# Second product of the last hidden blocks by seven products of quarters, after the first product

## The chip, the cores and the metric

The kernel runs on one core of one Trainium2 chip. The metric is device microseconds of one execution, the median of several runs; lower is better. A core has TensorE (PE, matmuls, with its weight loads shown apart as PEld), VectorE (DVE), ScalarE (ACT), GpSimd (POOL) and SyncE (SP), which issues most of the DMAs here. Each engine works through its own queue in order and waits on semaphores for the others.

## The reference

A transformer block over 2048 rows of 512 elements, in float32: LayerNorm, attention with 32 heads of 16 over 8 keys at a spacing of 2, an output product and a residual, then LayerNorm and an MLP with 1792 hidden elements and a squared ReLU, and a second residual.

```python
S, D, H, W, dil, F = 2048, 512, 32, 8, 2, 1792
def attention(x):                       # x: [S, D], 16 elements a head
    q, k, v = split_heads(x @ wqkv)
    # row s sees rows s, s-2, ..., s-14
    logits = einsum("hsd,hswd->hsw", q, k_window) * 16 ** -0.5
    return merge_heads(einsum("hsw,hswd->hsd", softmax(masked(logits)), v_window)) @ wo
def mlp(x):
    r = relu(x @ w1 + b1)               # [S, F]
    return (r * r) @ w2 + b2
h = x + attention(layernorm(x))
out = h + mlp(layernorm(h))
```

## The kernel before

**Products in two parts.** Every float32 operand of a matmul is split in a high part (a cast to float32r, `hi`, on ACT) and a low part (the rest, `lo`, a subtraction on DVE or POOL). A product is the sum of three: high by high, low by high, high by low. `mm3` does this for the products ahead of the MLP.

**Passes.** Rows are handled in four groups of 512 (R = 4 tiles of 128). After the products for q, k and v, the MLP runs in four passes u = 0 to 3, one for each group. In the first three the attention and the output product of the next group run beside it on the other engines. The change lies in the last pass, u = 3, which has nothing to run ahead for.

**The last pass before.** The hidden elements are 14 blocks f of 128, taken in seven pairs (`PAIRS`, (2, 9) first and (4, 11) last). The *first product* (r = relu(h w1 + b1), transposed, 128 hidden x 512 rows) is done for a pair by Winograd's form of Strassen's method: seven products of quarters in place of eight, 6 matmuls of 256 columns each. `products_a(n)` issues four of them (24 matmuls), `products_b(n)` three (18); the quarters are summed up in four PSUM banks (`XB`). The sums of w1's quarters come from `t_load(n)` (four DMAs into `traw`), `t_sums(n)` (four additions, on DVE for n < 2, else on POOL) and `t_split(n)` (one cast `th` on ACT, then two low parts `tl`, of w1's rows 256 to 511 first). In `products_b`, product 7 adds into the bank that u of `products_a` was computed from, so it comes after that DVE addition.

Of the result, `rest` and `second` make the squared ReLU of the pair's two blocks, and `squared` splits it into `rh` and `rl`. The *second product* of one block f (`mlp2`, called by `second_product`) is 12 matmuls of 512 columns: four tiles j, three terms, into four accumulators `acc[0..3]`. The high parts of w2 all lie in SBUF; of the low parts, 4 to 6 do, and `fetch` brings others from DRAM as places come free. After the seventh pair the last blocks' second products run tile by tile, `finish` adds the accumulator to the residual h (brought back from DRAM by `unspill`) and stores the tile, and `last_tile` does the last tile in two halves.

**What sets the order.** Everything is written out in program order per engine. The loop over n issues TensorE's work directly; other work is put on lists by `at(delta, fn, ...)`, "in the slot that is delta from now", and run by `end_slot` in the order in which it was put there. Each n has two slots, one after `products_a` and its second product, one after `products_b`. Row tiles of [128, 512] come from one tag with 15 buffers.

Of the kernel before, what the change touches and what calls it, by code (L numbers as in the profile page):

```python
# [20 lines left out]
RI = 2  # L21
# [9 lines left out]
LAG = 3  # L31
# [27 lines left out]
def block_kernel(ctx, tc, x, wqkv, wo, w1, b1, w2, b2, out):  # L59
    nc = tc.nc  # L60
# [20 lines left out]
    out_v = out.rearrange("o (b p i e) d -> (o b) e i p d", b=2, p=P, i=R, e=2)  # L81
# [26 lines left out]
    due = {}  # L108
# [4 lines left out]
    def at(delta, fn, *a):  # L113
        due.setdefault(now["slot"] + delta, []).append((fn, a))
# [7 lines left out]
    def end_slot(pe):  # L122
        now["pe"] += pe
        run(due)
        pump()
        run(amid)
        run(late)
        now["slot"] += 1

    def run(chores):  # L130
        todo = chores.get(now["slot"], [])
        while todo:
            fn, a = todo.pop(0)
            fn(*a)
# [16 lines left out]
    def hi(dst, src):  # L151
        nc.scalar.copy(dst, src)  # L152

    def lo(eng, dst, src, h):
        eng.tensor_tensor(out=dst, in0=src, in1=h, op=ALU.subtract)  # L155
# [438 lines left out]
    hs, hn = {}, {}  # L594
# [199 lines left out]
    def t_load(n):  # L794
        f = PAIRS[n][0]
        tw[n] = t_tile(n, "traw")
        for k in range(KB):
            nc.sync.dma_start(tw[n][:, k], bass.AP(
                tensor=w1.tensor, offset=w1.offset + k * P * F + f * P,
                ap=[[F, P], [F // 2, 2], [1, P]]))  # L800
# [39 lines left out]
    HD = D // 2  # L840
    pairs = {}

    def products_a(n):
        b = {m: psum.tile([P, D], F32, name="mm", tag=tag)[:, :HD]
             for m, tag in zip((1, 4, 2, 3), XB)}
        pu = row("p"), row("u")
        pairs[n] = b, pu
        for m, bank in ((1, 1), (4, 4), (6, 2), (5, 3)) if not n else ((1, 1), (6, 2), (5, 3), (4, 4)):
            product(n, m, b[bank], True, m == 4)
        nc.scalar.copy(pu[0][:, :HD], b[1])  # L850
        if not n:
# [3 lines left out]
        nc.vector.tensor_tensor(out=pu[1][:, :HD], in0=b[2], in1=pu[0][:, :HD], op=ALU.add)
        nc.scalar.copy(pu[0][:, HD:], b[3])

    def products_b(n):
        b, (p, u) = pairs[n]
        f, g = PAIRS[n]  # L860
        for m, bank in ((2, 1), (7, 2), (3, 3)):
            product(n, m, b[bank], False, True)
        rf, rg = row("r"), row("r")
        pairs[n] = rg
        tt = nc.vector.tensor_tensor
        nc.scalar.activation(rf[:, :HD], b[1], AF.Relu, bias=b1_sb[:, f:f + 1])
        tt(out=u[:, HD:], in0=b[2], in1=p[:, :HD], op=ALU.add)
        tt(out=rf[:, HD:], in0=u[:, HD:], in1=b[4], op=ALU.subtract)
        nc.gpsimd.tensor_tensor(out=rg[:, HD:], in0=u[:, HD:], in1=p[:, HD:], op=ALU.add)
# [10 lines left out]
        squared(g, rg)  # L880

    def squared(f, r):
        rh, rl = work.tile([P, D], F32R, name="rh", bufs=LAG + 1), row("rl", dt=F32R)
        nc.scalar.activation(r, r, AF.Square)
# [28 lines left out]
    def mlp2(u, f, acc, js, first=False, last=False, mid=None):  # L913

        rh, rl = hid[u, f]
        terms = [(rh, w2_h, j) for j in js] + [(rh, w2_l, j) for j in js]
        if len(js) > 1:
            terms += [(rl, w2_h, j) for j in js]
        else:
            terms.insert(1, (rl, w2_h, js[0]))  # L920
        for n, (l, w, j) in enumerate(terms):
            if mid and n == len(terms) // 2:
                mid()
            nc.tensor.matmul(acc[j], l[:, j * P:(j + 1) * P], w[f],  # L924
                             start=(first and n < len(js)),
                             stop=(last and n >= len(terms) - len(js)))
# [9 lines left out]
    def last_tile(t, fs):  # L936


        u, i = divmod(t, R)
        b, e = divmod(u, 2)  # L940
        h = hs.pop(t)
        js = slice(i * P, (i + 1) * P)
        for c, eng in ((slice(0, D // 2), nc.sync), (slice(D // 2, D), nc.scalar)):
            ps = turn["tr"].tile("half")[:, :D // 2]
            terms = [(f, l, w) for f in fs for l, w in ((0, w2_h), (1, w2_h), (0, w2_l))]
            for n, (f, l, w) in enumerate(terms):
                nc.tensor.matmul(ps, hid[u, f][l][:, js], w[f][:, c], start=(n == 0),  # L947
                                 stop=(n == len(terms) - 1))
            nc.vector.tensor_tensor(out=h[:, c], in0=ps, in1=h[:, c], op=ALU.add)  # L949
            eng.dma_start(out_v[b, e, i, :, c], h[:, c])  # L950
# [148 lines left out]
    place = {}  # L1099
# [121 lines left out]
    def second_product(last=False):  # L1221
        q = used[0]
        f = fs[q]
        if last:
            mlp2(u, f, acc, js[:-1])
            mlp2(u, f, acc, js[-1:], False, True)
        else:
            mlp2(u, f, acc, js, q == 0)
        used[0] += 1
# [29 lines left out]

    h = hs[S // P - 1]  # L1260
    for j in js[:-1]:
        for f in fs[-2:]:
            mlp2(u, f, acc, [j], False, f == fs[-1])
            if j == 0:
                end_slot(0.65)
        at(0, finish, R * u + j, acc[j])
        if j == 1:
            at(0, nc.vector.tensor_tensor, h, acc[-1], h, ALU.add)
        if j:
            run(due)  # L1270
# [24 lines left out]
```

## Time and profile before

| | |
|---|---|
| median of three runs | 501.18 us (501.14 to 502.29) |
| the profiled execution | 500.91 us, span 499.1 us |
| busy: PE, PEld | 99%, 84% |
| busy: DVE, ACT | 77%, 61% |
| instructions: PE, DVE, ACT, POOL | 2411, 526, 543, 429 |
| last pass, first matmul to last | 421.88 to 495.92 us in the span |
| granted clock of TensorE | 1.000 |

The profile's rows have the line of the kernel, the engine, the operation, `out<-in` by the program's names and the shapes. In the timeline the first two numbers are start and length in us, and in brackets stands the idle time of the engine before the instruction, with what ended it. A row may cover several instructions (xN). Matmuls overlap: a matmul's length is longer than the spacing of two. In the chain of work that ended last, a row has the start and length of a stretch of the chain.

### The profile page before, as it was taken

The numbers are of one execution on the slowest core, as the hardware profiler recorded it, in microseconds if no ns is written. First come the engines' busy times: TensorE is split into PE (matmuls) and PEld (weight loads), VectorE is DVE, ScalarE is ACT, GpSimd is POOL, SyncE is SP. The second block draws the span as 40 slices with busy tenths as digits, with TensorE's granted clock in tenths as the row PEclk, the third lists the DMA queues.
The fourth block names the chain that finished last, engine by engine and source line by source line (L and its number), as shares of the span: only waits on it lengthen the run. The fifth ranks groups of instructions, "written<-read, shape, count | busy, mean of one in ns | idle before, by whom it ended". The sixth has DMA issues, their size and how long they took to land.

```text
span 499.1 us, 7514 instructions
## 1 busy us (share of the span) xinstructions
PE 494.2 (99%) x2411; PEld 420.6 (84%) x2411; DVE 383.7 (77%) x526; ACT 305.7 (61%) x543; POOL 354.6 (71%) x429
## 2 busy tenths in 40 slices
PE   8999999999999999999999999999999999999997
PEld 7998888888888888888888888888888888998986
DVE  6479899999989989998979989897984257733233
ACT  4634778668346757478564556866454968766551
POOL 5714798996775999888878777787889353885610
PEclk9999999999999999999999999999999999999999
DMA  8779979889788899689776945977680575355212
GB/s 269 201 215 244 281 253 297 272 268 310 209 219 260 294 286 259 185 226 248 219 253 210 218 143 164 269 236 258 201 202 14 130 193 163 117 158 169 64 42 87
DMA packets 113584, 103.67 MB, mean 208 GB/s; under 512 B 33672, under 2 KB 82056, under 8 KB 113544
## 3 DMA queue, kind: packets, MB, share of 16 engines
q1 hardware_dynamic: 112600, 102.66, 70.1%
q10 hardware_dynamic: 944, 0.52, 0.3%
q8 instruction: 19, 0.31, 0.3%
q14 instruction: 21, 0.17, 0.1%
HBM read 72.65 MB, written 24.25 MB: 194 GB/s over the span
## 4 chain that ended last, share of the span: by engine, by line
PE 98%; DMA 1%; ACT 0%; ACTq 0%; DVE 0%; issue 0%
PE mm L231 49%; PE acc L924 30%; PE wo L231 9%; PE mm L837 7%; PE tr L204 2%; DMA wraw<-in_A_wqkv_dram 1%; PE half L947 0%; ACTq L570 0%; ACT big_h L152 0%; ACT xh L152 0%; DVE h L949 0%
## 5 line engine op out<-in xcount | busy, mean ns | idle before, releaser
L414 POOL TENSOR_TENSOR pr<-pr 128x512 f32<-128x512 f32 (+1 forms) x128 | 134.1, 1048 | 35.6 <-DVE pr L357 30.2
L231 PE MATMUL mm<-big_l,w_h 128*128 128x512 f32 x336 | 88.5, 390 | 0.0
L357 DVE TENSOR_TENSOR pr<-ex,v 128x1024 f32<-128x1024 f32 x62 | 75.6, 1221 | 12.0 <-POOL o L414 9.2
L344 DVE TENSOR_TENSOR pr<-qp,k 128x1024 f32<-128x1024 f32 x64 | 76.8, 1200 | 6.1 <-ACT qp L271 3.3
L380 DVE TENSOR_REDUCE ex<-pr 128x64 f32<-128x1024 f32 x64 | 78.4, 1225 | 1.8
L231 PEld LDWEIGHTS mm<-big_l,w_h 128*128 128x128 f32 x336 | 63.0, 188 | 13.4 <-ACT r L894 0.3
L155 POOL TENSOR_TENSOR rl<-r,rh 128x512 fp32r<-128x512 f32 x42 | 54.9, 1306 | 24.2 <-ACT rh L152 20.1
L231 PE MATMUL mm<-big_l,xh 128*128 128x512 f32 (+1 forms) x208 | 56.3, 379 | 0.0
L231 PE MATMUL mm<-big_h,xh 128*128 128x512 f32 (+1 forms) x208 | 53.1, 377 | 0.3 <-ACT xh L152 0.3
L231 PE MATMUL mm<-big_h,xl 128*128 128x512 f32 (+1 forms) x208 | 52.6, 374 | 0.0
L924 PE MATMUL acc<-big_h,rh 128*128 128x512 f32 x190 | 52.1, 391 | 0.0
L924 PE MATMUL acc<-big_l,rh 128*128 128x512 f32 x190 | 52.0, 390 | 0.0
L924 PE MATMUL acc<-big_h,rl 128*128 128x512 f32 x190 | 51.7, 390 | 0.0
L231 PE MATMUL mm<-big_l,w_l 128*128 128x512 f32 x168 | 44.9, 389 | 0.0
L231 PEld LDWEIGHTS mm<-big_h,xl 128*128 128x128 f32 x208 | 38.3, 188 | 6.0
L231 PEld LDWEIGHTS mm<-big_h,xh 128*128 128x128 f32 x208 | 37.9, 188 | 6.1 <-ACT xh L152 0.5
L924 PEld LDWEIGHTS acc<-big_h,rl 128*128 128x128 f32 x190 | 35.7, 188 | 7.4
L924 PEld LDWEIGHTS acc<-big_l,rh 128*128 128x128 f32 x190 | 35.6, 188 | 7.4
L231 PEld LDWEIGHTS mm<-big_l,xh 128*128 128x128 f32 x208 | 37.4, 188 | 4.9
L924 PEld LDWEIGHTS acc<-big_h,rh 128*128 128x128 f32 x190 | 35.1, 188 | 7.1 <-DVE h L932 0.3
L894 ACT ACTIVATE r<-mm,b_sb 128x512 f32<-128x512 f32 x42 | 28.7, 684 | 16.2 <-PE mm L231 15.7
L231 PEld LDWEIGHTS mm<-big_l,w_l 128*128 128x128 f32 x168 | 31.5, 188 | 6.6
(167 smaller groups left out, 919.4 us busy)
## 6 DMA issues: line engine op xcount, KB each, us to landing
k<-qkv_d SPq DMA_DIRECT2D x50, 288.0 KB, 3.2
v<-qkv_d SPq DMA_DIRECT2D x46, 288.0 KB, 3.2
qkv_d<-y SPq DMA_DIRECT2D x18, 512.0 KB, 4.0
big_l<-w2l_d SPq DMA_DIRECT2D x24, 256.0 KB, 3.1
xt<-in_A_x_dram SPq DMA_DIRECT2D x16, 256.0 KB, 4.2
q<-qkv_d SPq DMA_DIRECT2D x32, 128.0 KB, 3.6
h<-in_A_x_dram SPq DMA_DIRECT2D x16, 256.0 KB, 3.3
h_d<-h SPq DMA_DIRECT2D x16, 256.0 KB, 3.4
```

The lines of the kernel that those rows point to most:

```text
L155: eng.tensor_tensor(out=dst, in0=src, in1=h, op=ALU.subtract)
L204: nc.tensor.transpose(tr[:, k, :], src[:, k * P:(k + 1) * P], ident)
L231: nc.tensor.matmul(ps, l(k), r(k), start=(n == 0), stop=(n == 3 * KB - 1))
L344: nc.vector.tensor_tensor(out=pr.rearrange("p i w h d -> p i w (h d)"), in0=qps["now"][:, j % 2].unsqueeze(2).to_broadcast([P, RI, W, GC]) ...
L357: nc.vector.tensor_tensor(out=p2, in1=vwin, op=ALU.mult, in0=e1[:, :, :, j * GH:(j + 1) * GH].unsqueeze(4).to_broadcast([P, RI, W, GH, DH]))
L380: nc.vector.tensor_reduce(out=lf[:, :, :, j * GH:(j + 1) * GH], in_=pr, axis=X, op=ALU.add)
L414: nc.gpsimd.tensor_tensor(out=dst, in0=p2[:, :, :w], in1=p2[:, :, w:2 * w], op=ALU.add)
L837: nc.tensor.matmul(ps, sta[y][:, k], mov[x][:, k], start=(first and q == 0), stop=(last and q == len(terms) - 1), skip_group_check=True)
L894: nc.scalar.activation(r, ps, AF.Relu, bias=b1_sb[:, f:f + 1])
L924: nc.tensor.matmul(acc[j], l[:, j * P:(j + 1) * P], w[f], start=(first and n < len(js)), stop=(last and n >= len(terms) - len(js)))
```

## The change

The last three pairs, (0, 7), (1, 8) and (4, 11), are taken out of the second product's row of blocks, and their second product is also done by seven products of quarters. For each pair the stationary side is r (2 blocks of hidden elements by two halves of the rows) and the moving side w2 (2 blocks by two halves of the columns). This needs:

- sums of w2's quarters: `v_load(q)` loads the two blocks of w2 again, as `vraw`; `v_sums(q)` makes four sums (DVE for q = 0 and 1, POOL for q = 2); `v_split(q)` makes two casts and two low parts. Loads are issued in n = 1, 2 and 4 (`VS`), the sums in the second slot of the same n, the split in the second slot of the next;
- sums of r's quarters: `s_sums(n)` (four on DVE), `s_split(n)` (two casts on ACT, two low parts on DVE);
- all parts of r in the last pass now lie in columns of w1's parts that their own pair has used, not in tiles of their own (`parted`).

The eight other blocks keep their wide second product, one in each n from 1 to 6, one more in n = 5 (`PLAN`, first number: after `products_a`, second: after `products_b`), and one after the last `products_b`. Then come `outer(n)` for the three pairs (products 1, 6, 5, 7, into the four banks of the first product), and `inner` (product 4 into the left halves of `acc[2]` and `acc[3]`); products 3 and 2 of tiles 0 and 1 come last, and the last half tile goes into a bank of its own, `z`. The four outer results are summed up on ACT and DVE and added to h by POOL and DVE beside these. The `unspill` loads move from n = 4 and 5 to behind the first `outer`.

```diff
+WN = 3
+PLAN = {1: (1, 0), 2: (1, 0), 3: (1, 0), 4: (1, 0), 5: (1, 1), 6: (1, 0)}
+VS = {1: 0, 2: 1, 4: 2}
+VP = range(2)
...
-        rh, rl = work.tile([P, D], F32R, name="rh", bufs=LAG + 1), row("rl", dt=F32R)
         nc.scalar.activation(r, r, AF.Square)
-        hi(rh, r)
-        lo(nc.vector, rl, r, rh)
-        hid[R - 1, f] = rh, rl
+        rh, rl = [w[:, :, f * P:(f + 1) * P] for w in (w1_h, w1_l)]
+        parted(f, r)
+    def parted(f, r):
+        rh, rl = [w[:, :, f * P:(f + 1) * P] for w in (w1_h, w1_l)]
+        n = RI if f in WINO[:WN] else R
+        src = r.rearrange("p (j c) -> p j c", j=R)[:, :n]
+        hi(rh[:, :n], src)
+        lo(nc.vector, rl[:, :n], src, rh[:, :n])
+        hid[R - 1, f] = [lambda j, a=a: a[:, j] for a in (rh, rl)]
+    def v_sums(q):
+        (b11, b12), (b21, b22) = [(r[:, :HD], r[:, HD:]) for r in vw[q]]
+        tt, sub = (nc.vector if q in VP else nc.gpsimd).tensor_tensor, ALU.subtract
+        tt(out=b11, in0=b12, in1=b11, op=sub)
+        tt(out=b12, in0=b22, in1=b12, op=sub)
+        tt(out=b22, in0=b22, in1=b11, op=sub)
+        tt(out=b21, in0=b21, in1=b22, op=sub)
+    def s_split(n):
+        for x, f in zip(whole.pop(n), PAIRS[n - PLAIN]):
+            src = x.rearrange("p (j c) -> p j c", j=R)
+            h, l = [w[:, :, f * P:(f + 1) * P] for w in (w1_h, w1_l)]
+            hi(h, src)
+            lo(nc.vector, l, src, h)
+    def part(n, m, ps, js, first=False, last=False):
...
+        terms = [(x, y, j) for x, y in ((0, 0), (1, 0), (0, 1)) for j in js]
+        for k, (x, y, j) in enumerate(terms):
+            nc.tensor.matmul(ps[j], sta[x][:, i0 + j], mov[y], start=first and k == 0,
+                             stop=last and k >= len(terms) - len(js), skip_group_check=True)
...
     for n in range(len(PAIRS)):
         if n + 2 < len(PAIRS):
             t_load(n + 2)
+        if n in VS:
+            v_load(VS[n])
         products_a(n)
...
             at(0, second, n - 1)
+            if n > PLAIN:
+                at(0, s_sums, n - 1)
             if n + 1 < len(PAIRS):
                 at(0, t_split, n + 1)
-            second_product()
-        if n in (4, 5):
-            for i in range(2):
-                at(0, unspill, R * u + 2 * (n - 4) + i)
+            for _ in range(PLAN[n][0]):
+                second_product()
         end_slot(5.6)
         products_b(n)
         if n + 2 < len(PAIRS):
             at(0, t_sums, n + 2)
-        if n > 1:
+        if n in VS:
+            at(0, v_sums, VS[n])
+            at(2, v_split, VS[n])
+        if n > PLAIN:
+            at(0, s_split, n - 1)
+        for _ in range(PLAN[n][1] if n else 0):
             second_product()
         if n == len(PAIRS) - 1:
             at(0, second, n)
-            second_product(True)
+            at(0, s_sums, n)
+            at(0, s_split, n)
+            for i in js:
+                at(1, unspill, R * u + i)
+            while used[0] < len(fs):
+                second_product()
         end_slot(4.9)
...
-    last_tile(S // P - 1, fs[-2:])
+    for n in range(head, end):
+        outer(n)
+    inner(head, 4)
+    outer(end)
+    tt = nc.vector.tensor_tensor
+    v, u2, u3, s12, s22 = [row("c") for _ in range(5)]
+    nc.scalar.copy(v, two[1])
+    tt(out=u2, in0=two[6], in1=v, op=ALU.add)
...
+    for eng, i, cs, src in ((nc.gpsimd, 0, left, v), (nc.gpsimd, 1, left, v),
+                            (nc.gpsimd, 2, left, u3), (nc.gpsimd, 3, left, u3),
+                            (nc.vector, 2, right, s22), (nc.vector, 3, right, s22),
+                            (nc.gpsimd, 0, right, s12), (nc.gpsimd, 1, right, s12)):
...
+    for n in range(head + 1, end + 1):
+        inner(n, 4)
+    for i in (2, 3):
+        finish(R * u + i, acc[i])
+    z = psum.tile([P, D], F32, name="part", tag=XB[0])[:, left]
+    for m, j, ps in ((3, 0, acc[0][:, right]), (2, 0, acc[0][:, left]),
+                     (3, 1, acc[1][:, right]), (2, 1, z)):
+        for n in range(head, end + 1):
+            part(n, m, [ps, ps], [j], ps is z and n == head, n == end)
+        if m == 2 and not j:
+            finish(R * u, acc[0])
...
+    tt(out=h, in0=acc[1], in1=h, op=ALU.add)
+    nc.scalar.dma_start(out_v[b, e, 1, :, right], h[:, right])
+    tt(out=h[:, left], in0=z, in1=h[:, left], op=ALU.add)
+    nc.sync.dma_start(out_v[b, e, 1, :, left], h[:, left])
```

Here `PLAIN` is 4, the number of pairs left to the wide second product, `head` is 4 and `end` is 6, and `WINO` lists the last three pairs' first blocks, then their second ones.

More of the change, by code (lines that the diff above doesn't have):

```diff
@@ L865, in products_b @@
         tt = nc.vector.tensor_tensor
+        if n >= PLAIN:
+            whole[n] = rf, rg
         nc.scalar.activation(rf[:, :HD], b[1], AF.Relu, bias=b1_sb[:, f:f + 1])
@@ new lines, in block_kernel, with v_load @@
+    hid = {}
+    PLAIN = len(PAIRS) - WN
+    WINO = [p[i] for i in range(2) for p in PAIRS[PLAIN:]]
+    whole, vw = {}, {}
+    def v_load(q):
+        vw[q] = row("vraw"), row("vraw")
+        for r, f in zip(vw[q], PAIRS[PLAIN + q]):
+            nc.sync.dma_start(r, w2[f * P:(f + 1) * P, :])
+    def v_sums(q):
[5 more added lines that the diff above has]
+        tt(out=b21, in0=b21, in1=b22, op=sub)
@@ new lines, in v_split @@
+    def v_split(q):
+        if q == 0:
+            t = [work.tile([P, D], F32R, name="rh", bufs=LAG + 1) for _ in range(4)]
+        elif q == 1:
+            t = [att.tile([P, D], F32R, name="vs", tag=tag) for tag in ("k", "k", "v", "v")]
+        else:
+            t = [a[:, i] for a in [att.tile([P, 2, D], F32R, name="vs", tag="o", bufs=3)
+                                   for _ in range(2)] for i in range(2)]
+        raw = vw[q]
+        vw[q] = t[:2], t[2:]
+        for i in range(2):
+            hi(t[i], raw[i])
+            lo(nc.vector, t[2 + i], raw[i], t[i])
@@ new lines, in s_sums @@
+    def s_sums(n):
+        rf, rg = whole.pop(n)
+        (a11, a21), (a12, a22) = [(r[:, :HD], r[:, HD:]) for r in (rf, rg)]
+        x = whole[n] = row("x"), row("x")
+        tt, sub = nc.vector.tensor_tensor, ALU.subtract
+        tt(out=x[0][:, :HD], in0=a21, in1=a22, op=ALU.add)
+        tt(out=x[1][:, :HD], in0=a11, in1=a21, op=sub)
+        tt(out=x[0][:, HD:], in0=x[0][:, :HD], in1=a11, op=sub)
+        tt(out=x[1][:, HD:], in0=a12, in1=x[0][:, HD:], op=sub)
+    def s_split(n):
[4 more added lines that the diff above has]
+            lo(nc.vector, l, src, h)
@@ new lines, in part @@
+    def part(n, m, ps, js, first=False, last=False):
+        q, (f, g) = n - PLAIN, PAIRS[n]
+        c, d = PAIRS[q]
+        col, i0 = {1: (f, 0), 2: (g, 0), 4: (g, 2), 5: (c, 0), 6: (c, 2), 7: (d, 0), 3: (d, 2)}[m]
+        sta = [w[:, :, col * P:(col + 1) * P] for w in (w1_h, w1_l)]
+        lo_, hi_ = slice(0, HD), slice(HD, D)
+        if m < 4:
+            w, cs = f if m == 1 else g, hi_ if m == 3 else lo_
+            mov = w2_h[w][:, cs], w2_l[w][:, cs]
+        else:
+            i, cs = {5: (0, lo_), 7: (0, hi_), 4: (1, lo_), 6: (1, hi_)}[m]
+            mov = [t[i][:, cs] for t in vw[q]]
+        terms = [(x, y, j) for x, y in ((0, 0), (1, 0), (0, 1)) for j in js]
+        for k, (x, y, j) in enumerate(terms):
+            nc.tensor.matmul(ps[j], sta[x][:, i0 + j], mov[y], start=first and k == 0,
+                             stop=last and k >= len(terms) - len(js), skip_group_check=True)
@@ L896, in hidden @@
         hi(rh, r)
-        at(wait, lo, nc.vector if u == R - 1 else nc.gpsimd, rl, r, rh)
-        hid[u, f] = rh, rl
+        at(wait, lo, nc.gpsimd, rl, r, rh)
+        hid[u, f] = [lambda j, a=a: a[:, j * P:(j + 1) * P] for a in (rh, rl)]
     def hidden_now():
@@ L923, in mlp2 @@
                 mid()
-            nc.tensor.matmul(acc[j], l[:, j * P:(j + 1) * P], w[f],
+            nc.tensor.matmul(acc[j], l(j), w[f],
                              start=(first and n < len(js)),
@@ L934, in finish @@
         nc.sync.dma_start(out_v[b, e, i], h)
[L936 to L950, printed above, removed]
     def flush():
@@ L1213, in block_kernel @@
     now["sub"] = u
-    fs = [f for pair_ in PAIRS for f in pair_]
-    need = [f for f in fs if f < 12 and f not in place]
+    fs = [f for pair_ in PAIRS[:PLAIN] for f in pair_]
+    need = [f for f in fs + WINO if f < 12 and f not in place]
     acc = [psum.tile([P, D], F32, name="acc", tag=tag) for tag in ("acc0", "acc1", "tr0", "tr1")]
@@ L1219, in block_kernel, with refill @@
     used = [0]
[L1221 to L1229, printed above, removed]
+    def refill(f):
         if f < 12 and need:
@@ L1232, in second_product @@
             at(1, fetch, need.pop(0))
+    def second_product():
+        q = used[0]
+        mlp2(u, fs[q], acc, js, q == 0, q == len(fs) - 1)
+        used[0] += 1
+        refill(fs[q])
     for n in range(len(PAIRS)):
@@ L1256, in block_kernel @@
             at(0, second, n)
-            second_product(True)
-        end_slot(4.9)
[L1260 to L1270, printed above, removed]
-    last_tile(S // P - 1, fs[-2:])
+            at(0, s_sums, n)
@@ new lines, in block_kernel, with outer @@
+            at(0, s_split, n)
[3 more added lines that the diff above has]
+                second_product()
+        end_slot(4.9)
+    two = {m: psum.tile([P, D], F32, name="part", tag=tag) for m, tag in zip((1, 5, 6, 7), XB)}
+    halves = {m: [t[:, j * HD:(j + 1) * HD] for j in range(RI)] for m, t in two.items()}
+    both, left, right = range(RI), slice(0, HD), slice(HD, D)
+    head, end = PLAIN, len(PAIRS) - 1
+    def outer(n):
+        for m in (1, 6, 5, 7) if n < end else (1, 6, 7, 5):
+            part(n, m, halves[m], both, n == head, n == end)
+        refill(PAIRS[n][0])
+        run(due)
+        now["slot"] += 1
@@ new lines, in inner @@
+    def inner(n, m):
+        part(n, m, [acc[RI + j][:, left] for j in both], both, False, n == end)
+    for n in range(head, end):
[6 more added lines that the diff above has]
+    tt(out=u2, in0=two[6], in1=v, op=ALU.add)
+    tt(out=u3, in0=two[7], in1=u2, op=ALU.add)
+    tt(out=s22, in0=two[5], in1=u3, op=ALU.add)
+    tt(out=s12, in0=two[5], in1=u2, op=ALU.add)
@@ new lines, in block_kernel @@
+    for eng, i, cs, src in ((nc.gpsimd, 0, left, v), (nc.gpsimd, 1, left, v),
+                            (nc.gpsimd, 2, left, u3), (nc.gpsimd, 3, left, u3),
+                            (nc.vector, 2, right, s22), (nc.vector, 3, right, s22),
+                            (nc.gpsimd, 0, right, s12), (nc.gpsimd, 1, right, s12)):
+        h = hs[R * u + i][:, cs]
+        eng.tensor_tensor(out=h, in0=h, in1=src[:, i % RI * HD:(i % RI + 1) * HD], op=ALU.add)
+    for n in range(head + 1, end + 1):
+        inner(n, 4)
@@ new lines, in block_kernel @@
+    for i in (2, 3):
[7 more added lines that the diff above has]
+            finish(R * u, acc[0])
+    h = hs.pop(R * u + 1)
+    b, e = divmod(u, 2)
+    tt(out=h, in0=acc[1], in1=h, op=ALU.add)
```

## Prediction

> **What bounds the kernel now.** I read the page's totals first, then the chain of work that ended last over the final pass, then the timeline of each queue in that pass, and last the groups of instructions by form. n is the index of a pair in `PAIRS`, "a(n)" and "b(n)" are the 24 and 18 matmuls of `products_a` and `products_b`, "m7" is product 7.
>
> ```profile
> span 499.1 us, 7514 instructions
> PE 494.2 (99%) x2411; PEld 420.6 (84%) x2411; DVE 383.7 (77%) x526; ACT 305.7 (61%) x543; POOL 354.6 (71%) x429
> ...
> PE 98%; DMA 1%; ACT 0%; ACTq 0%; DVE 0%; issue 0%
> ```
>
> TensorE is the bound, POOL has the next longest queue beside it in this pass, and the chain never leaves TensorE there:
>
> ```profile
> 440.71 2.15 PE mm L837 x18
> 442.87 2.75 PE acc L924 x12
> 445.61 2.87 PE mm L837 x24
> ...
> 484.94 9.55 PE acc L924 x42
> 494.49 1.44 PE half L947 x12
> ...
> 495.96 0.42 DVE h L949
> ```
>
> From here come my prices: 18 or 24 matmuls of 256 columns take 2.15 or 2.87 us, 0.1195 each; the 12 of 512 columns of one second product take 2.75, the step between widths included. So a saving in matmuls is a saving in time, as long as TensorE still finds every operand ready. Before, each pair's 42 narrow matmuls have two second products beside them (10.5 us a pair); afterwards pairs 2, 3 and 4 have one: 5.02 + 2.75 = 7.77 us. So I looked for the work that must end once per pair, and where it was late already:
>
> ```profile
> 434.25 0.33 SPq L697 DMA_DIRECT2D h_d<-h  x1
> 434.67 2.53 SPq L798 DMA_DIRECT2D traw<-in_B_w_dram  x4
> 437.30 0.54 SPq L697 DMA_DIRECT2D h_d<-h  x1
> ```
> ```profile
> 438.18 0.85 POOL L805 TENSOR_TENSOR traw<-traw 128x256 f32<-128x256 f32 x1 [0.30 <-DMA traw<-in_B_w_dram]
> 439.49 0.74 POOL L806 TENSOR_TENSOR traw<-traw 128x256 f32<-128x256 f32 x1 [0.46 <-DMA traw<-in_B_w_dram]
> 440.31 1.06 POOL L807 TENSOR_TENSOR traw<-traw 128x256 f32<-128x256 f32 x1
> 441.45 0.74 POOL L808 TENSOR_TENSOR traw<-traw 128x256 f32<-128x256 f32 x1
> 443.35 2.56 POOL L155 TENSOR_TENSOR tl<-traw,th 128x512 fp32r<-128x512 f32 x2 [1.16 <-ACT th L152]
> 445.85 1.20 POOL L869 TENSOR_TENSOR r<-u,p 128x256 f32<-128x256 f32 x1
> 447.01 0.74 POOL L805 TENSOR_TENSOR traw<-traw 128x256 f32<-128x256 f32 x1
> ...
> 449.47 0.74 POOL L808 TENSOR_TENSOR traw<-traw 128x256 f32<-128x256 f32 x1
> 451.37 2.55 POOL L155 TENSOR_TENSOR tl<-traw,th 128x512 fp32r<-128x512 f32 x2 [1.16 <-ACT th L152]
> 453.88 0.74 POOL L869 TENSOR_TENSOR r<-u,p 128x256 f32<-128x256 f32 x1
> ```
> ```profile
> 442.22 1.05 ACT L152 CAST th<-traw 128x1024 fp32r<-128x1024 f32 x1 [2.27 <-DMA traw<-in_B_w_dram]
> ```
>
> The reader is to see POOL's round for one pair: four sums of the raw quarters (`t_sums`), a wait for ACT's cast `th`, two low parts `tl`, then one addition of the pair before. From the end of `tl` of pair 3 (443.35 + 2.56 = 445.91) to that of pair 4 (451.37 + 2.55 = 453.92) it takes 8.01 us. Against 10.5 us of TensorE it is hidden; against 7.77 it is the longer one. And pair 3 starts late: its raw weights leave SP only at 434.67, behind a spill, and POOL waits for them twice.
>
> **The change part by part.**
>
> *TensorE.* The second product of six hidden blocks, 72 wide matmuls, becomes 7 products x 6 narrow x 3 pairs = 126. Before, ten second products stand ahead of the end of b(6), and 11.14 us follow it (484.78 to 495.92, the last matmul's end): 10 x 2.75 + 11.14 = 38.64. After: seven ahead, one behind, and 126 x 0.1195 = 15.06, with 0.16 for the last one's drain: 8 x 2.75 + 15.22 = 37.22. Saved: 1.4 us. This is all that can be gained; `last_tile` went into it.
>
> *The end.* As before, a 256-column addition and one 128 KB store follow the last matmul; cost 0. The eight additions into h, four sums of `two` and four `finish`-like additions lie beside the last 7.2 us of matmuls (42 in outer(6) and both late inners, 36 after them): POOL has six of about 0.74 (its row L869, 453.88), done some 4.5 us after product 1 of outer(6), 1.7 before the addition to tile 1 wants the last. Cost 0, a microsecond if that cover fails.
>
> *Pair 3 comes sooner.* The second product between b(2) and a(3) is gone. These rows give the places:
>
> ```profile
> 440.55 0.40 PE L837 MATMUL mm<-big_l,w_h 128*128 128x256 f32 x2
> ...
> 441.26 0.40 PE L837 MATMUL mm<-wo_h,th 128*128 128x256 f32 x2
> ...
> 442.70 1.09 PE L924 MATMUL acc<-big_h,rh 128*128 128x512 f32 x4
> ```
> ```profile
> 466.49 0.40 PE L837 MATMUL mm<-big_l,w_h 128*128 128x256 f32 x2
> ...
> 468.16 0.40 PE L837 MATMUL mm<-wo_h,tl 128*128 128x256 f32 x2
> ```
>
> b(2) starts at 440.55 with the same work ahead of it in both kernels. a(3) would follow at 442.70 and reach the second `tl` 1.67 later (466.49 to 468.16), at 444.37. POOL delivers it at 445.91: at least 1.54 us of standstill, by rows that nothing in the change makes earlier.
>
> *`v_load(0)` and `v_sums(0)`.* Its two loads stand in SP's queue behind `traw` of pair 3 (434.67 + 2.53 = 437.20), ahead of the spill, a fetch of w2's low part and `traw` of pair 4. Its sums stand on DVE ahead of u of pair 2, and m7 of b(2) writes over the bank that u reads.
>
> ```profile
> big_l<-w2l_d SPq DMA_DIRECT2D x8, 256.0 KB, 2.9
> ```
> ```profile
> 438.36 0.41 DVE L855 TENSOR_TENSOR u<-mm,p 128x256 f32<-128x256 f32 x1
> 440.04 0.73 DVE L155 TENSOR_TENSOR rl<-r,rh 128x512 fp32r<-128x512 f32 x1 [1.28 <-POOL traw L805]
> ```
> ```profile
> L784 DVE TENSOR_TENSOR s<-pl 128x256 f32<-128x256 f32 x2 | 0.8, 418 | 0.0
> L884 ACT ACTIVATE r<-r 128x512 f32<-128x512 f32 x14 | 8.9, 633 | 0.4
> L152 ACT CAST rh<-r 128x512 fp32r<-128x512 f32 x14 | 8.7, 621 | 0.4
> L155 DVE TENSOR_TENSOR rl<-r,rh 128x512 fp32r<-128x512 f32 x14 | 11.3, 807 | 23.7 <-ACT rh L152 19.0 <-POOL traw L808 2.6 <-POOL traw L805 1.3
> ```
>
> Issued at 437.2 and 437.6, landed 2.9 later, 440.1 and 440.5; four sums of 0.42 end near 442.2, u near 442.65 instead of 438.77. m7, due at 441.26 (the second row above), starts near 442.7, 1.4 late. The other delay runs through POOL: its addition at 440.31 took 1.06 and not 0.74 while DVE's op of 440.04 ran (0.73, in the rows ahead), 0.32 more; by that share four DVE sums add about 0.2 each, less the 0.32 already there: `tl` ends at about 446.4. The two delays overlap: 446.4 + 0.1 - 444.37 = 2.1 us. Bounds: 1.54, and 2.9 if the loads land 0.8 later in a queue that is moving data all that time. I take 2.1.
>
> The Trainium skill, page "SBUF — State Buffer", section "Who interferes with whom", says that a DVE instruction with two SBUF inputs and a GpSimd instruction that reads SBUF exclude each other, the later one standing still until the first is done. The trace agrees in direction: 1.06 for 0.74, though 0.32 is less than DVE's whole 0.73.
>
> *Pairs 4 and 5.* After pair 3 TensorE and POOL leave together, so each pair costs the difference of their rounds: 8.01 - 7.77 = 0.24 as a floor. Pair 4's round has `v_sums(1)` beside it, up to 4 x 0.2: 0.24 to 1.0; I take 0.6, because some of these fall where POOL waits for `th` (its 1.16 us). Pair 5's has the two low parts of `v_split(1)`, up to 2 x 0.32: 0.24 to 0.9, taken 0.5. ACT's additions (`v_split`, 2 x 0.62 a pair) come before `th` in its queue. The row of pair 3's stretch before, whose columns are TensorE, weight loads, DVE, ACT and POOL:
>
> ```profile
> 445.42:455.94 10.52, 10.52 (x67) 9.54 (x66) 3.80 (x7) 5.91 (x10) 9.05 (x11) 1.00 0.37 113
> ```
>
> ACT gets to 5.91 + 1.24 = 7.15 of 7.77 us and stays inside; POOL, with 9.05 busy, does not.
>
> *Pair 6.* `PLAN[5]` leaves two second products: TensorE's round is 10.52. POOL loses the wait for `th` but gets `v_sums(2)`, four more at 0.82 from start to start (447.01 to 449.47 is three): 8.01 - 1.16 + 3.28 = 10.13, and up to 0.8 from `s_sums(4)` on DVE: 0 to 0.4, taken 0.1.
>
> *The parts of r behind the first product.* Removed: `rl`'s rows. Added a pair: 1.5 more casts and low parts, four sums. After b(6) the order is `rest(6)`, `s_split(5)`, `second(6)`, `s_sums(6)`, `s_split(6)`. By the rows above: eight ACT operations of 0.63 (5.0), a low part 0.7, four sums 1.7, a cast 0.6 and two low parts 1.4: the last near 9.4 us after b(6). TensorE has one second product, two outers and an inner, 2.75 + 2 x 2.87 + 0.72 = 9.2, and wants the last part 1.44 later, at 10.65. Hidden, by 1.2; up to 1 us if pair 6 leaves ACT behind. That r's parts go into columns of w1 costs 0 as well: product 3 has read those columns by then, and a cast into one part of a weight tile holds no matmul on its other parts, as at the kernel's start, where both are `big_h`:
>
> ```profile
> 16.02 0.93 ACT L152 CAST big_h<-wraw 128x384 fp32r<-128x384 f32 x2
> 16.48 0.85 PE L231 MATMUL mm<-big_h,xl 128*128 128x384 f32 x4
> ```
>
> If it did hold them, each of 13 handovers would cost a cast and a low part, some 1.4 us; I give that no chance of its own. The four moved `unspill` loads go out behind outer(4), over 10 us before use.
>
> **Sum.** 2.1 + 0.6 + 0.5 + 0.1 - 1.4 = +1.9 us. The profiled execution took 500.91, which is 0.27 under the median of 501.18, so 502.8 against it, 503.1 against the median. The bounds: 1.54 + 0.24 + 0.24 - 1.4 = +0.6, or 501.8; 2.9 + 1.0 + 0.9 + 0.4 + 1 - 1.4 = +4.8, or 506.0.
>
> **Rivals.**
> 1. *All hidden (not slower).* If pair 3's second `tl` were there by 444.37, every later round would start with slack, and TensorE's 1.4 remain: 499.8. For it: 1.5 us is little for an engine that is busy 71% of the span. Against: the rows of SP and POOL, which stand before anything new. It decides at 444.37.
> 2. *Late once only.* Pair 3 costs 1.54 to 2.1 and POOL then keeps up at 7.6 (rounds without any slowed op: 0.74 + 3.2 + 1.16 + 2.55): +0.1 to 0.7, 501.6. For it: four of its ten ops above ran undisturbed. Against: 8.01 was measured with fewer DVE ops beside it.
> 3. *DVE and POOL exclude each other for whole instructions.* Then `v_sums(1)` adds 4 x 0.42 = 1.67 to POOL's round, `v_split(1)` 2 x 0.73, `s_sums(4)` 1.67: 0.24 + 1.67, 0.24 + 1.46 and 10.13 + 1.67 - 10.52, together 4.9, with 2.6 for pair 3, less 1.4: +6.1, 507.3. That is the skill's rule just named, taken whole. Against: 0.32 measured, not 0.7.
> 4. *The tail.* The parts of pair 6 come 1.5 to 3 us after they are wanted: on top of the forecast some 505. Against: the margin of 1.2.
>
> **How the numbers follow.** A measurement of this kernel tells 0.3%, 1.5 us, from no change: 499.7 and 502.7. Chances: the forecast 0.55, rival 1 0.13, rival 2 0.20, rival 3 0.07, rival 4 0.05. Some 0.10 of the forecast lies under 502.7. Slower: 0.45 + 0.07 + 0.05 = 0.57; faster: half of rival 1, 0.06; same: 0.37. Predicted 503.1, its own range 501.8 to 506.0; for 8 in 10 I reach to the hidden case: 499.9 to 506.0.
>
> **What would show it.** Right: TensorE's first idle time in the final pass, at m7 of b(2) behind DVE's u, and at the second `tl` of pair 3; smaller ones at the same place in pairs 4 and 5; POOL's `tl` starting within 1.3 us of `th` and ending just before TensorE goes on; `v_sums(0)` waiting for `vraw`. About 37.2 us of TensorE for the work priced above. Wrong: no idle TensorE before a(3); or idle at outer(5) or outer(6), which would be rival 4; or POOL's sums at 1.1 to 1.5 us each, which would be rival 3.

## The result

The changed kernel takes 505.27 us (median), the kernel before 501.48 in the same sets of runs: a ratio of 1.0083, with a 95% interval of 1.007 to 1.0095. It is slower by 4 us. One of the six executions of the kernel before took 2848.61 us and is in that median; without it the median is 501.18. The prediction was 503.1, with a range of 499.9 to 506.0.

The page of the changed kernel: span, busy time of each engine, and the chain of work that ended last.

```profile
span 504.4 us, 7694 instructions
...
PE 494.9 (98%) x2459; PEld 422.6 (84%) x2459; DVE 410.4 (81%) x563; ACT 311.2 (62%) x556; POOL 366.5 (73%) x439
...
PE 76%; POOL 8%; ACT 5%; DMA 4%; issue 3%; SPq 1%; DVE 1%; POOLq 0%; ACTq 0%
```

The chain has left TensorE: 98% became 76%, and POOL, ACT and DMA hold most of the rest. These shares say where the chain runs, not how much time is lost: TensorE is still busy for 98% of the span. The timeline of TensorE, final pass only, shows where. These are all its rows with idle time, after its first narrow matmul:

```profile
422.63 0.40 PE L841 MATMUL mm<-big_l,w_h 128*128 128x256 f32 x2
...
444.40 0.50 PE L841 MATMUL mm<-wo_h,th 128*128 128x256 f32 x2 [2.25 <-DVE u L859]
...
453.70 0.50 PE L841 MATMUL mm<-wo_h,th 128*128 128x256 f32 x2 [1.26 <-DVE u L859]
...
463.65 0.50 PE L841 MATMUL mm<-big_l,w_h 128*128 128x256 f32 x2 [0.47 <-ACT r L872]
...
465.88 0.51 PE L841 MATMUL mm<-wo_h,tl 128*128 128x256 f32 x2 [0.27 <-POOL tl L159]
...
476.89 0.50 PE L841 MATMUL mm<-wo_h,tl 128*128 128x256 f32 x2 [0.23 <-POOL tl L159]
```

An idle stretch costs more than the bracket says, since a matmul's shown length (0.28) is over its spacing (0.12) and the row after a wait has 0.34 to the next instead of 0.24. From start to start the losses are 2.51 (product 7 of pair 2), 1.52 (product 7 of pair 3), 0.73 and 0.57 (pair 5), 0.49 (pair 6): 5.8 us.

From here on "the last pass" is the time from the start of its first narrow matmul to the start of the last addition: 495.96 - 421.88 = 74.08 before, 501.14 - 422.63 = 78.51 after. The difference, 4.43, is 5.8 less 1.4 of matmuls. The profiled execution of the changed kernel took 506.15, the longest of its six; 0.75 of it (422.63 for 421.88) lies ahead of the changed code, and no later variant's profile shows that much.

What the first two waits stand on, in DVE's timeline of the changed kernel (its last row is the last addition):

```profile
441.37 0.45 DVE L918 TENSOR_TENSOR vraw<-vraw 128x256 f32<-128x256 f32 x1 [2.17 <-DMA vraw<-in_B_w_dram]
442.15 0.54 DVE L919 TENSOR_TENSOR vraw<-vraw 128x256 f32<-128x256 f32 x1 [0.34 <-DMA vraw<-in_B_w_dram]
...
443.93 0.41 DVE L859 TENSOR_TENSOR u<-mm,p 128x256 f32<-128x256 f32 x1
...
446.55 2.50 DVE L159 TENSOR_TENSOR rh<-vraw,rh 128x512 fp32r<-128x512 f32 x2
448.98 1.23 DVE L159 TENSOR_TENSOR w_l<-r,w_h 128x512 fp32r<-128x512 f32 x1
450.13 0.96 DVE L918 TENSOR_TENSOR vraw<-vraw 128x256 f32<-128x256 f32 x1
451.13 0.84 DVE L919 TENSOR_TENSOR vraw<-vraw 128x256 f32<-128x256 f32 x1
...
453.23 0.42 DVE L859 TENSOR_TENSOR u<-mm,p 128x256 f32<-128x256 f32 x1
...
501.14 0.42 DVE L1380 TENSOR_TENSOR h<-part,h 128x256 f32<-128x256 f32 x1 [0.33 <-PE part L968]
```

u of pair 2 (443.93) waits behind sums whose data land late; u of pair 3 (453.23) waits behind seven operations with no idle time between them (three low parts and four sums), and all but the last sum are longer than alone: 1.25 and 1.23 for a low part (0.69), 0.84 to 0.96 for a sum (0.42). Beside them POOL's timeline:

```profile
448.47 1.19 POOL L809 TENSOR_TENSOR traw<-traw 128x256 f32<-128x256 f32 x1
449.74 1.07 POOL L810 TENSOR_TENSOR traw<-traw 128x256 f32<-128x256 f32 x1
450.89 0.80 POOL L811 TENSOR_TENSOR traw<-traw 128x256 f32<-128x256 f32 x1
...
453.73 2.94 POOL L159 TENSOR_TENSOR tl<-traw,th 128x512 fp32r<-128x512 f32 x2 [1.16 <-ACT th L156]
```

Both engines are stretched while both work: POOL's sums 0.80 to 1.19 for 0.74, its two low parts 2.94 for 2.53.

### The profile page after: what moved, and what is told of

Read it like the earlier page. It is cut to its first block, busy times and chain, and to the rows that moved or that the text cites. A ratio compares the mean times of both kernels' runs of the same rounds, so it can differ in the third digit from the quotient of the medians.

```text
span 504.4 us, 7694 instructions
## 1 busy us (share of the span) xinstructions
PE 494.9 (98%) x2459; PEld 422.6 (84%) x2459; DVE 410.4 (81%) x563; ACT 311.2 (62%) x556; POOL 366.5 (73%) x439
## 4 chain that ended last, share of the span: by engine, by line
PE 76%; POOL 8%; ACT 5%; DMA 4%; issue 3%; SPq 1%; DVE 1%; POOLq 0%; ACTq 0%
PE mm L235 45%; PE acc L1004 18%; PE wo L235 7%; PE tr L208 2%; DMA o<-pl 2%; POOL tl L159 2%; PE part L968 2%; DMA traw<-in_B_w_dram 2%; ACT pl L642 2%; PE acc L968 1%; SPq L802 1%; PE tr L1041 1%; ACT pl L633 1%; POOL pr L418 1%; POOL traw L811 1%
## 5 line engine op out<-in xcount | busy, mean ns | idle before, releaser
L1004 PE MATMUL acc<-big_l,rh 128*128 128x512 f32 x144 | 38.7, 390 | 0.0
L1004 PE MATMUL acc<-big_h,rl 128*128 128x512 f32 x144 | 38.5, 389 | 0.0
L1004 PE MATMUL acc<-big_h,rh 128*128 128x512 f32 x144 | 38.5, 389 | 0.0
L540 ACT COPY y<-mm 128x512 f32<-128x512 f32 x36 | 21.0, 584 | 24.2 <-PE mm L235 20.8
L418 POOL TENSOR_TENSOR o<-pr 128x128 f32<-128x128 f32 x64 | 30.9, 482 | 5.0
L1004 PEld LDWEIGHTS acc<-big_h,rl 128*128 128x128 f32 x144 | 27.0, 188 | 5.6
```

Of the source, the lines that this page charges most:

```text
L418: nc.gpsimd.tensor_tensor(out=dst, in0=p2[:, :, :w], in1=p2[:, :, w:2 * w], op=ALU.add)
L1004: nc.tensor.matmul(acc[j], l(j), w[f], start=(first and n < len(js)), stop=(last and n >= len(terms) - len(js)))
```

## The experiments

The table has medians, with the ratio to the kernel before in the same set of runs (its medians lie between 500.82 and 501.48) and its 95% interval, and the last pass of the profile.

| run | us | ratio to before | last pass |
|---|---|---|---|
| before | 501.18 | 1 | 74.08 |
| changed | 505.27 | 1.0083 (1.007 to 1.0095) | 78.51 |
| e1 columns alone | 501.04 | 1.0000 (0.9991 to 1.0009) | 74.06 |
| e2 thin cover alone | 503.84 | 1.0051 (1.0036 to 1.0066) | 76.91 |
| e3 sums behind u | 505.04 | 1.0074 (1.0059 to 1.0089) | 78.34 |
| e4 no sums on DVE | 504.83 | 1.0074 (1.0056 to 1.0092) | 77.75 |
| e5 first low part on DVE | 503.70 | 1.0048 (1.0033 to 1.0063) | 76.51 |
| e6 and cover at pair 3 | 505.08 | 1.0078 (1.0063 to 1.0093) | 78.45 |
| e7 and all w2 sums on DVE | 502.55 | 1.0026 (1.0016 to 1.0036) | 75.48 |
| e8 no w1 sums on POOL | 500.10 | 0.9978 (0.9968 to 0.9987) | 72.71 |
| e9 DVE's work spread | 501.33 | 1.0010 (1.0001 to 1.0019) | 74.44 |
| e10 spread, other way | 501.76 | 1.0019 (1.0010 to 1.0028) | 74.90 |
| e11 no tail cover | 503.20 | 1.0046 (1.0032 to 1.0061) | 75.96 |
| e12 later sums | 500.75 | 0.9994 (0.9985 to 1.0003) | 73.53 |

**e1: r's parts in columns of w1, nothing else.**

```diff
-        rh, rl = work.tile(...), row("rl", dt=F32R)
+        rh, rl = [w[:, :, f * P:(f + 1) * P] for w in (w1_h, w1_l)]
```

> The kernel before with one part of the change alone: r's parts of the last pass are written into used columns of the first weights, and the second product reads them there. Everything else stays as it was. Theory (the standstill comes from thinner cover and from the added sums): no difference, within 0.3 us of the kernel before. Rival (casts into the columns hold back matmuls that read other columns of the same weights): at least 1 us slower, with idle TensorE in products_a or products_b behind a cast or a low part.

The same as before, and no row of TensorE's timeline with idle time in the last pass. This part of the change costs nothing.

**e2: thin cover alone.** It holds e1's edit. Wide second products throughout, but placed as in the changed kernel.

```diff
+PLAN = {1: (1, 0), 2: (1, 0), 3: (1, 0), 4: (1, 0), 5: (1, 1), 6: (1, 0)}
...
-            second_product()
+            for _ in range(PLAN[n][0]):
+                second_product()
```

> As e1, and the wide second products stand where the changed kernel has them (one in each n from 1 to 6, one more in n = 5), the other seven behind the first product; no sums of w2 or of r. TensorE's work is that of the kernel before. Theory: POOL's round alone is too long for the thinner cover; TensorE stands still at the low part tl of pair 3 for 1.5 to 2 us and for 0.2 to 0.5 us each at pairs 4 and 5: about 2.2 us slower than before (1.5 to 3). Rival (only the added work causes the standstill): as fast as before within 0.3 us.

2.7 us slower, with not one instruction of the new products. All rows with idle time in TensorE's last pass in this run:

```profile
443.73 0.50 PE L838 MATMUL mm<-big_l,w_h 128*128 128x256 f32 x2 [0.98 <-ACT r L867]
...
445.95 0.51 PE L838 MATMUL mm<-wo_h,tl 128*128 128x256 f32 x2 [0.26 <-POOL tl L156]
...
454.28 0.50 PE L838 MATMUL mm<-wo_h,tl 128*128 128x256 f32 x2 [0.27 <-POOL tl L156]
...
462.61 0.50 PE L838 MATMUL mm<-wo_h,tl 128*128 128x256 f32 x2 [0.28 <-POOL tl L156]
```

The last three rows stand at the same place, POOL's second low part of pairs 3, 4 and 5, and 8.33 us apart. TensorE needs 7.77 for a pair, so it has taken POOL's beat and loses 0.56 at pairs 4 and 5 each; the other 1.7 of the 2.83 are pair 3's. That is the size foreseen, but most of it is lost ahead of the low part, at the first product of the pair (443.73), which waits for ACT's r. In ACT's queue r stands behind `th`, and `th` waits for POOL's last sum, so this too is POOL's round:

```profile
442.25 1.05 ACT L153 CAST th<-traw 128x1024 fp32r<-128x1024 f32 x1 [2.41 <-POOL traw L809]
443.20 0.47 ACT L867 ACTIVATE r<-mm,b_sb 128x256 f32<-128x256 f32 x1
```

The 2.83 are about half of the 5.8 us of the changed kernel, and the rival that only added work counts falls.

**e3 and e4: the sums that stand ahead of u, moved or left out.**

```diff
-            at(0, v_sums, VS[n])
+            at(VS[n] in VP, v_sums, VS[n])                               # e3
+            at(0, v_sums, VS[n]) if VS[n] not in VP else None            # e4
```

> The changed kernel, with the sums of w2's quarters for q = 0 and 1 one slot later on DVE, so behind u of the next pair and not ahead of it. Theory (DVE's order costs the 2.5 and 1.5 us at product 7 of pairs 2 and 3, but POOL's late low parts stand behind it): both waits on u go, and TensorE waits at tl of pair 3 for about 1.7 us and of pair 4 for about 0.7 instead: 1.6 us faster than the changed kernel (0.8 to 2.5). Rival (POOL is the limit all through, and DVE's wait only hides it): no faster than the changed kernel by more than 0.3 us.

> The changed kernel without the eight DVE additions that form the sums of w2's quarters for q = 0 and 1 (these additions are left out; the loads, casts and low parts stay). Theory: no wait on u; TensorE waits at tl of pair 3 for about 1.5 us, at that of pair 4 for about 0.3, since POOL loses less time to DVE: 2.3 us faster than the changed kernel (1.5 to 3). Rival (DVE and POOL exclude each other for whole instructions): 3 us faster or more, with POOL's sums of pairs 4 and 5 back at 0.74 us each.

Both theories missed; e3 came out as its rival had it, e4 as neither. The waits on u go in both, but e3 is only 0.2 us under the changed kernel and e4 0.4. From TensorE's rows of e3:

```profile
443.74 0.50 PE L841 MATMUL mm<-big_l,w_h 128*128 128x256 f32 x2 [1.06 <-ACT r L872]
...
446.95 0.51 PE L841 MATMUL mm<-wo_h,tl 128*128 128x256 f32 x2 [0.73 <-POOL tl L159]
...
456.02 0.51 PE L841 MATMUL mm<-wo_h,tl 128*128 128x256 f32 x2 [0.72 <-POOL tl L159]
...
464.81 0.50 PE L841 MATMUL mm<-wo_h,tl 128*128 128x256 f32 x2 [0.27 <-POOL tl L159]
```

and of e4:

```profile
443.90 0.50 PE L841 MATMUL mm<-big_l,w_h 128*128 128x256 f32 x2 [0.89 <-ACT r L872]
...
446.58 0.51 PE L841 MATMUL mm<-wo_h,tl 128*128 128x256 f32 x2 [0.71 <-POOL tl L159]
...
455.79 0.51 PE L841 MATMUL mm<-wo_h,tl 128*128 128x256 f32 x2 [0.71 <-POOL tl L159]
```

The wait has moved to POOL's low part and, at pair 3, to ACT's r; from pair 3 to pair 4 the low parts are 9.07 us apart in e3 and 9.21 in e4. So DVE's order, the cause that the largest bracket names, was a wait in front of another of nearly the same end. My first theory, that the waits on u are worth 1.6 us or more by themselves, fell. The new one: a pair's round over POOL, and DVE beside it, is longer than TensorE's 7.77; e2 has 8.33 of it without new work, and what DVE adds stretches it to 8.8 to 9.3.

e4 also says which of DVE's additions do this. It leaves the eight sums out, and the round is still 9.21. What DVE has there beyond e2 are the low parts of `v_split`. The rows of POOL and DVE in e4:

```profile
452.76 2.97 POOL L159 TENSOR_TENSOR tl<-traw,th 128x512 fp32r<-128x512 f32 x2 [1.16 <-ACT th L156]
455.70 1.18 POOL L875 TENSOR_TENSOR r<-u,p 128x256 f32<-128x256 f32 x1
```
```profile
453.60 2.68 DVE L159 TENSOR_TENSOR vs<-vraw,vs 128x512 fp32r<-128x512 f32 x2
```

Beside these two low parts, POOL's two take 2.97 and the addition behind them 1.18; in e2 they take 2.55 and 0.73. No run leaves `v_split` out, so this share is read from rows, not tested.

**e8: POOL's sums of w1 left out.** To see what is left when POOL's round is short; it leaves out the sums for pairs 2 to 6 and holds e3's edit.

```diff
-            at(0, t_sums, n + 2)
+            pass
```

> As e3, without the sums of w1's quarters for pairs 2 to 6, which are POOL's (these additions are left out; loads, casts and low parts stay). Theory: POOL's round falls to about 5 us and TensorE waits nowhere, so this shows what the matmuls save: 499.8 (499.5 to 500.4), 1.4 us under the kernel before. Rival (the narrow matmuls on columns of the first weights run slower, or the end waits): 500.8 or more with no wait on POOL in the trace.

As the theory had it: no idle row in the last pass, 500.1, and a last pass 1.37 us under that before. Its DVE rows, to be set against the sums of the changed kernel at 450.13 and 451.13:

```profile
446.44 0.41 DVE L918 TENSOR_TENSOR vraw<-vraw 128x256 f32<-128x256 f32 x1
446.89 0.43 DVE L919 TENSOR_TENSOR vraw<-vraw 128x256 f32<-128x256 f32 x1
```

The same two additions take 0.41 and 0.43 instead of 0.96 and 0.84 when POOL is not adding beside them.

**e5, e6, e7: POOL's work to DVE, and the cover moved.** Each holds the edit of the one before; all hold e3's.

```diff
-        for k, eng in ((2, nc.vector if n < 3 else nc.gpsimd), (0, nc.gpsimd)):
+        for k, eng in ((2, nc.vector), (0, nc.gpsimd)):                  # e5
-PLAN = {..., 2: (1, 0), ..., 5: (1, 1), 6: (1, 0)}
+PLAN = {..., 2: (1, 1), ..., 5: (1, 0), 6: (1, 0)}                       # e6
-VP = range(2)
+VP = range(3)                                                            # e7
```

> As e3 (sums of w2 behind u), and DVE takes the first low part tl of every pair, POOL only the second (before: DVE only up to pair 2). POOL's round for one pair, 8.3 to 9.2 us in e3, loses about 1.3 to 1.5 us. Theory (POOL's round against TensorE's 7.77 us is the standstill): pairs 4 and 5 wait 0.2 us or less each, pair 6 not at all, pair 3 about 2 us as before since its weights and sums are late: 503.0 (502.3 to 503.8), so about 2 us faster than e3. Rival (DVE is as full as POOL, and the two hold each other up): no faster than e3 by more than 0.5 us.

> As e5, and the extra second product stands behind products_b(2), not behind products_b(5). Theory: the 2.75 us of cover take in all that pair 3 waits for; pair 6, whose round on POOL holds the four sums of w2 for q = 2, now waits 1 to 1.5 us: 501.0 (500.3 to 501.8). Rival (pair 3's lateness is only passed on to pair 4, since POOL gains nothing by TensorE's later start): waits of 0.5 to 1 us at pairs 4 and 5 as well, 502.5.

> As e6, and the four sums of w2 for q = 2 on DVE, behind u, and not on POOL. Theory: POOL's round at pair 6 is that of pairs 4 and 5, and TensorE waits nowhere for more than 0.2 us: 500.0 (499.7 to 500.6), at or just over the 1.4 us under the kernel before that the matmuls save. Rival (DVE becomes the bound at pairs 5 and 6, with some 8 us of work a pair): TensorE waits for DVE there, 501.5 or more.

e5 lies within its range, with a gain of 1.3 against e3, not 2: the waits for POOL's second low part are gone, and product 4 of pairs 3 and 4 waits 0.94 and 0.91 for DVE's u instead, which now stands behind `tl` in DVE's queue. e6 loses the gain again and lies above its theory and its rival. From its TensorE and DVE rows:

```profile
473.70 0.51 PE L841 MATMUL mm<-big_l,th 128*128 128x256 f32 x2 [2.38 <-DVE u L873]
```
```profile
470.35 0.96 DVE L944 TENSOR_TENSOR x<-x,r 128x256 f32<-128x256 f32 x1
471.34 1.37 DVE L945 TENSOR_TENSOR x<-r,x 128x256 f32<-128x256 f32 x1
472.63 0.68 DVE L159 TENSOR_TENSOR tl<-traw,th 128x512 fp32r<-128x512 f32 x1
473.23 0.41 DVE L873 TENSOR_TENSOR u<-mm,p 128x256 f32<-128x256 f32 x1
```

Pair 3's waits are gone, but pair 6 has lost its cover and waits 2.4 us, now for DVE: r's sums beside POOL's sums of w2 take 0.95 to 1.37 each, `tl` comes behind them, and the addition that frees product 4's bank behind that. I had counted only POOL there. But that wait only takes the place of those at pair 3 in e5. What makes e6 slower than e5 comes behind it: shortly after this stretch, its longest idle one, TensorE runs at half its clock for some 3 us. In these rows the columns are the stretch, its length, TensorE, weight loads, DVE, ACT, POOL, then the granted clock:

```profile
475.00:477.00 2.00, 2.00 (x11) 2.00 (x11) 1.76 (x5) 1.97 (x6) 0.00 (x0) 0.50 0.00 0
477.00:479.00 2.00, 2.00 (x8) 1.58 (x7) 0.93 (x2) 1.94 (x5) 0.00 (x0) 0.66 0.00 0
479.00:481.00 2.00, 2.00 (x13) 1.77 (x12) 1.64 (x4) 0.27 (x1) 0.00 (x0) 1.00 0.16 25
```

From 473.70 to the second four matmuls of the next second product it takes 4.78 us; the same matmuls take 3.25 in e7, where the clock stays at 1.00. So about 1.5 us of e6's 505.1 are the clock's. All four executions of e6 show the same mean clock, 0.997. The changed kernel kept 1.00 after an idle stretch of 2.25 us; why 2.38 us had this effect is not shown.

With those sums on DVE (e7) POOL is free, r's sums fall to 0.41 for three of the four, and the wait to 1.15; 0.89 stay at pair 4. Of the 2.5 us that e7 gains on e6, some 1.5 are the clock. e7 still misses its theory and meets its rival, DVE as the bound.

**e9, e10, e12: DVE's work spread.** e9 loads w2 for q = 1 in n = 3 and puts `s_sums(4)` into the second slot of n = 5; e10 has the same place for `s_sums(4)`, leaves q = 1 and gives pair 4's first low part to POOL; e12 is e9 with `v_sums(2)` and `v_split(2)` later.

```diff
-VS = {1: 0, 2: 1, 4: 2}
+VS = {1: 0, 3: 1, 4: 2}                                                  # e9, e12
...
+        for k, eng in ((2, nc.gpsimd if n == 4 else nc.vector), (0, nc.gpsimd)):   # e10
...
+        if n == PLAIN + 1:                                               # all three
+            at(0, s_sums, n - 1)
+            at(1, s_split, n - 1)
...
-            at(VS[n] in VP, v_sums, VS[n])
-            at(2, v_split, VS[n])
+            at(1 + (n == 4), v_sums, VS[n])                              # e12
+            at(2 + 2 * (n == 4), v_split, VS[n])
```

> As e7, with DVE's new work spread out: w2's quarters for q = 1 are loaded in n = 3 (sums and split one pair later), and r's sums of the first of the three pairs come in the second slot of n = 5, their split in the first of n = 6. e7's two waits for DVE (product 4 of pairs 4 and 6, some 1.0 and 1.3 us) have DVE's queue behind them. Theory: both go, no wait is over 0.3 us, and the last pass is within 0.6 us of the 72.7 that e8 took: 500.2 (499.7 to 500.9). Rival (DVE is full over pairs 3 to 6 as a whole, the waits only move): 501.5 or more.

> As e7, with r's sums of the first of the three pairs as late as in e9, and the first low part of pair 4 back on POOL, q = 1 as in e7. Theory: DVE's wait of pair 4 goes and a wait for POOL's second low part of that pair takes its place, about 0.4 us: 500.4 (499.8 to 501.2). Rival as in e9: 501.5 or more.

> As e9, with the sums of w2 for q = 2 half a pair later again (second slot of n = 5) and their split in the second slot of n = 6, so that the low part of pair 6 on DVE isn't behind them. Theory: e9's wait at product 4 of pair 6 (0.65 us idle) goes; u of pair 6 and the tail come up to 0.5 us later than in e9: 500.7 (500.2 to 501.3), about 0.5 us under e9 and level with the kernel before. Rival (the wait moves to product 7 of pair 6 or to outer(6)): no faster than e9.

e9 lies between theory and rival, e10 within its rival: one wait went, smaller ones stayed (0.65 at pair 6 and 0.23 at pair 5 in e9; 0.72 on POOL's `tl` of pair 4 in e10, and two of about 0.2). e12 came out as expected: it removes e9's wait at pair 6. Against e8 its last pass is still 0.82 longer; from start to start about half of that is at product 4 of pair 5 and half at the tail, in its chain of work:

```profile
487.01 0.70 DVE w_l L159
487.72 0.04 issue
487.76 2.17 PE part L968 x16
```

e12's last pass is 0.55 us under that before, and its time, at a ratio whose interval reaches over 1, cannot be told from it. No version here that does all the work beats the kernel before for certain.

**e11: the tail without cover.** It holds e3's edit.

```diff
-PLAN = {..., 2: (1, 0), ..., 5: (1, 1), 6: (1, 0)}
+PLAN = {..., 2: (1, 1), ..., 5: (1, 1), 6: (1, 0)}
```

> As e3, with the one second product that stood between the last products_b and the first of the seven products of quarters moved to behind products_b(2). It tests the tail: r's parts of the last pairs have 2.75 us less cover there. Theory (about 1.2 us of slack at the tail in the changed kernel): the 2.75 us are saved as waits at pairs 3 to 6, and TensorE waits about 1.5 us at outer(6) for s_split: 503.8 (503.0 to 504.6). Rival (the tail has more slack than that): no wait at the tail, 502.3.

Within the range, and now the tail waits, for the part I named. One of TensorE's two rows there:

```profile
489.75 0.50 PE L968 MATMUL part<-vs,w_l 128*128 128x256 f32 x2 [0.22 <-DVE w_l L159]
```

From start to start the tail loses 0.87 us at product 6 of outer(6), not 1.5: the slack was 2.75 - 0.87 = 1.9, not 1.2.

## Why the prediction was right, and where its sizes were off

*TensorE saves 1.4 us.* Right: e8, without waits, is 1.37 under before. The unit prices from the chain's rows (0.1195 a narrow matmul) hold.

*The columns of w1, and the end: 0.* Right: e1, and in the changed kernel and e3 to e12 the last 48 matmuls run without a gap.

*The mechanism: POOL's round against a thinner cover.* Right, and shown by e2 (8.33 against 7.77), where I had read 8.01 from the rows of before.

*Pair 3, 2.1 us.* Measured 2.51. The place (product 7, behind u) was right; the loads landed 3.4 us after their issue (438.01 to 441.37), not 2.9. The second place named, `tl` of pair 3, shows no idle time in the changed kernel, because product 7's wait covers it. That POOL stands behind it was right as well: without the sums (e4), pair 3 still loses 0.89 at ACT's r and 0.71 at `tl` by the brackets.

*Pair 4, 0.6; pair 5, 0.5; pair 6, 0.1.* Measured 1.52, 1.30, 0.49. This is the step that failed. I charged DVE's new work to POOL, a sum at 0.2 and a low part at 0.32, and to nobody else. The rows show that DVE is stretched as well (0.96 for 0.42, 1.25 for 0.69), and that in its queue u comes behind: pair 4's loss was taken as a wait for DVE, which I had named for pair 2 only. POOL's share was wrong too. Its sums lose 0.06 each to DVE's sums (0.80 for 0.74), not 0.2. It is the low parts of `v_split` that lengthen its round, by 0.42 to 0.45 each in e4; I had charged those of q = 1 to pair 5 alone, and those of q = 0, which lie in pair 4's round (446.55), to no pair.

This is rival 3's condition: by the ends in the last section, the later of two such operations stands still until the first has ended. My reading against it, 0.32 measured and not 0.73, took the wrong length: DVE's operation ended at 440.77 (440.04 + 0.73), and POOL's addition ended 0.60 after that (440.31 + 1.06 = 441.37), the same 0.60 as in the rows there. Rival 3's price was wrong the other way, since it put DVE's whole length on POOL's round for every sum. My sum had 3.3 us of waits, rival 3 had 7.5, measured are 5.8.

*The tail, hidden by 1.2.* Hidden, by 1.9 as e11 measures it. My chain of ACT and DVE operations was 9.4 us; in the changed kernel b(6) ends at 483.09, and the last low parts in DVE's timeline 8.75 later:

```profile
490.55 1.29 DVE L159 TENSOR_TENSOR w_l<-x,w_h 128x512 fp32r<-128x512 f32 x2 [0.23 <-ACT w_h L156]
```

So the sum's sign and its main causes held, and the terms for two engines working side by side, 1.2 us for pairs 4 to 6, measured 3.3.

## What to carry to other kernels

When matmuls are taken from between other matmuls, what they saved must be set against the time that one round takes on every other engine over the same stretch: here the matmuls saved 1.4 us, and the thinner cover alone cost 2.83. Price added work on POOL and DVE together, as one resource where both inputs lie in SBUF: the later of two operations waits for the first, and so does whoever stands behind it in its queue. And the largest wait in a trace need not be the cause: take it away (e3, e4) before building on it.

## What the runs showed of the hardware

DVE additions with both inputs in SBUF and POOL additions run one after the other, but for a short piece. The ends show it (start plus length, from the rows of the changed kernel above). POOL's sum of 448.47 ends at 449.66; DVE's low part, started meanwhile, ends at 450.21, 0.55 later. Then POOL ends at 450.81 (0.60 later), DVE at 451.09 (0.28), POOL at 451.69 (0.60), DVE at 451.97 (0.28). Alone these operations take 0.69, 0.74 and 0.42. So in each case the last 0.55, 0.60 or 0.28 us follow the other engine's end, and only the first 0.14 lie under it.

This gives the price of alternating sums of 256 columns. In the changed kernel, from 450.9 to 452.9, each engine starts one every 0.88 us, which is 0.60 and 0.28. Alone POOL starts one every 0.82 (447.01 to 449.47 of the kernel before, three steps) and DVE every 0.45 (the rows of e8). So POOL loses 0.06 and DVE 0.43.

The Trainium skill, page "SBUF — State Buffer", section "Who interferes with whom", has the later of two such instructions standing still until the first is done. The runs agree, by these ends. Adding up the two intervals would give 1.27, more than the 0.88 measured, since the first 0.14 of a waiting instruction and the pauses between two of one engine lie under the other's work.

A DVE addition with one input in PSUM kept its length beside POOL: this one lies within POOL's low parts of 453.73 to 456.67.

```profile
454.72 0.42 DVE L873 TENSOR_TENSOR u<-mm,p 128x256 f32<-128x256 f32 x1 [0.48 <-PE mm L841]
```
